# Experts 1 to 6 of a mixture-of-experts kernel: seven block products for the second layer on two pairs of token tiles, in an order written out by hand

## Chip, cores and metric

The kernel runs on one core of a Trainium2 chip. The metric is the time of one execution on the device, in microseconds (us), as the median of the runs shown. The profile is of one execution. TensorE appears in it as PE (products) and PEld (weight loads), VectorE as DVE, ScalarE as ACT, GpSimd as POOL, and the queue that issues the loads from memory as SP.

## The reference, cut to what matters

Strided and local attention gives x, 1152 tokens by 512. A dense mixture of 8 experts follows, whose weights P are balanced by eight rounds over rows and columns (Sinkhorn), and then a mixture that sends each token to two of eight experts.

```python
P = np.exp(logits)
for _ in range(8):
    P /= P.sum(1, keepdims=True) + 1e-09
    P /= P.sum(0, keepdims=True) + 1e-09
    P *= N / E
for e in range(E):                      # 8 experts, w1 512x1024, w2 1024x512
    h = np.maximum(x @ w1[e], 0.0)
    ye = h @ w2[e]
    out += P[:, e:e + 1] * ye
return out.astype(np.float32)
```

The change lies in experts 1 to 6 of the dense mixture, in the end of the balancing, and in what prepares both.

## The kernel before

Every float32 factor of a large product is split in two fp32r parts: ACT writes the high part, DVE the rest (high minus source), and three products (high by high, high by low, low by high) are added in PSUM. `split` does one block of this, `mm3` (L171) the three products.

Attention comes first. Then expert 0 runs in four quarters of its 1024 hidden units, for all nine tiles of 128 tokens (`pair1`, `pair2`); during it the gate logits and all eight rounds of the balancing (`sinkhorn`, L397 to L409) run as a chain of small DVE instructions and one small product a round. GpSimd forms four sums of blocks of x (L683, L685), which `sums` splits in high and low (`sl<-r` on DVE).

Experts 1 to 6 follow in 24 quarters. A quarter is 256 hidden units of one expert. Its 1 MB of weights comes by one load (`fetch_u`, L140). `conv_wino` forms four differences of blocks of w1 on GpSimd (L161) and splits seven blocks; `conv_u2` splits the quarter's part of w2. The first layer is a two by two block product with seven block products (Winograd's form) in place of eight. Class `Unit` does it for a set of columns (tokens): products `p1` to `p7` of six instructions each (L730), sums between them on DVE in PSUM (L751, L755, L761), and relu with a split in gh and gl. Two units, each 288 columns in each half of the tokens, make up the 1152 tokens. The second layer is plain: `pair2` takes one tile of 128 tokens, six products 512 wide (tile y), and DVE adds the result times P to acc (L650); nine tiles make a quarter.

The order of the work on each engine is set by the tile scheduler from the order in which the code is written, except in stretches under `manual_schedule`, where the engine's instructions run as written. Before, the 24 quarters are left to the scheduler, and the stretch after them (expert 7 and the routing) is written by hand. PSUM has eight banks, four tags with two each.

After the quarters come expert 7 (`g1`, `g2`), the routing, and the second mixture (`up`, `Down`), which the change leaves as it is except for when two weight tiles of expert 7 are fetched and split (`load_w`, a0 and b0).

Of the kernel before, what the change touches and what calls it, by code (L numbers as in the profile page):

```python
# [21 lines left out]
NT = N // 128  # L22
# [4 lines left out]
SUB = HALF // 2  # L27
# [35 lines left out]
def tile_kernel(ctx: ExitStack, tc: tile.TileContext, qL, kL, vL, qS, kS, vS, wg, u12, w1, w2, wgn, noise, v1, v2, cst, masks, dummy, out):  # L63
# [91 lines left out]

    def conv_wino(raw):
        hi, lo = (upool.tile([128, 7, 2, 128], F32R, tag=t, name=t) for t in ("u1h", "u1l"))
        t = upool.tile([128, 4, 2, 128], F32, tag="ut", name="ut", bufs=1)
        b11, b21, b12, b22 = (raw[:, 2 * k:2 * k + 2, j * 128:(j + 1) * 128] for j in range(2) for k in range(2))
        for o, x, y in ((0, b12, b11), (2, b22, b12), (1, b22, t[:, 0]), (3, b21, t[:, 1])):  # L160
            nc.gpsimd.tensor_tensor(t[:, o], x, y, op=ALU.subtract)  # L161
        split(hi[:, :2].rearrange("p a b n -> p (a b) n"), lo[:, :2].rearrange("p a b n -> p (a b) n"), raw[:, :, :128])
        split(hi[:, 2], lo[:, 2], b22)
        split(hi[:, 3:], lo[:, 3:], t)
        return hi, lo
# [217 lines left out]
    def sinkhorn():  # L383
        mx = spool.tile([128, 1], F32, name="mx")
        nc.vector.tensor_reduce(mx, lg, axis=AX.X, op=ALU.max)
        p = ps("b", "mxT")
        nc.tensor.transpose(p[:1, :128], mx, ident)
        nmx = spool.tile([1, 1], F32, name="nmx1")
        nc.vector.tensor_reduce(nmx, p[:1, :128], axis=AX.X, op=ALU.max, negate=True)
        p = ps("b", "mxB")  # L390
        nc.tensor.matmul(p[:, :1], onesr[:1, :], nmx, start=True, stop=True)
        nmb = spool.tile([128, 1], F32, name="nmb")
        nc.vector.tensor_copy(nmb, p[:, :1])
        nc.scalar.activation(P.rearrange("p t e -> p (t e)"), lg, AF.Exp, bias=nmb)
        for _ in range(8):
            rs = spool.tile([128, NT], F32, name="rs")
            nc.vector.tensor_reduce(rs, P, axis=AX.X, op=ALU.add)  # L397
            nc.vector.tensor_scalar(rs, rs, 1e-9, None, op0=ALU.add)
            nc.vector.reciprocal(rs, rs)
            nc.vector.tensor_tensor(P, P, rs[:, :, None].to_broadcast([128, NT, E]), op=ALU.mult)  # L400
            c1 = spool.tile([128, E], F32, name="c1")
            nc.vector.tensor_reduce(c1, P.rearrange("p t e -> p e t"), axis=AX.X, op=ALU.add)
            p = ps("b", "cs")
            nc.tensor.matmul(p[:, :E], onesr, c1, start=True, stop=True)
            c2 = spool.tile([128, E], F32, name="c2")
            nc.vector.tensor_scalar(c2, p[:, :E], 1e-9, None, op0=ALU.add)
            nc.vector.reciprocal(c2, c2)
            nc.vector.tensor_scalar(c2, c2, float(N) / E, None, op0=ALU.mult)
            nc.vector.tensor_tensor(P, P, c2[:, None, :].to_broadcast([128, NT, E]), op=ALU.mult)  # L409
# [264 lines left out]
    quarter = [[x[:, 2 * k:2 * k + 2, m * HALF:(m + 1) * HALF] for m in range(2) for k in range(2)] for x in (xh, xl)]  # L674
# [4 lines left out]
    for c in range(2):  # L679
        r = tpool.tile([128, 4, HALF], F32, tag="r", name="r")  # L680
        blocks.append(r)
        for i in range(4):
            nc.gpsimd.tensor_tensor(r[:, i], quarter[0][i][:, c].bitcast(F32), quarter[1][i][:, c].bitcast(F32), op=ALU.add)  # L683
# [19 lines left out]
    with tc.issue_after(marks[1]), tc.issue_after(lows[0].ins):  # L703
        sums()
# [8 lines left out]
    XOP = [(quarter[0][i], quarter[1][i]) for i in (0, 1, 3)] + [(sh[:, i], sl[:, i]) for i in range(4)]  # L713
    A11, A12, A22, S1, S2, S3, S4 = XOP

    class Unit:
        def __init__(self, w, u):
            self.w, self.o = w, u * SUB
            self.bank = {}

        def product(self, k, b, x, first):
            if first:
                self.bank[k] = ps(k, k)
            p = self.bank[k][:, :SUB]
            wh, wl = self.w
            i = 0
            for c in range(2):
                r = [y[:, c, self.o:self.o + SUB] for y in x]
                for l, m in ((wh, r[0]), (wh, r[1]), (wl, r[0])):
# [4 lines left out]
        def keep(self, name, p):  # L734
            s = upool.tile([128, SUB], F32, tag=name, name=name)
            nc.scalar.activation(s, p, AF.Copy)
            return s

        def done(self, p, m, j):
            o = m * HALF + self.o  # L740
            split(gh[:, j, o:o + SUB], gl[:, j, o:o + SUB], p, relu=True)

        def p1(self):
            self.s1 = self.keep("s1", self.product("a", B11, A11, True))

        def p5(self):
            self.s5 = self.keep("s5", self.product("b", T1, S1, True))

        def p6(self):
            p = self.product("a", T2, S2, False)  # L750
            nc.vector.tensor_tensor(self.bank["b"][:, :SUB], p, self.s5, op=ALU.add)  # L751

        def p2(self):
            p = self.product("d", B21, A12, True)
            nc.vector.tensor_tensor(p, p, self.s1, op=ALU.add)  # L755
            self.done(p, 0, 0)

        def p7(self):
            p = self.product("a", T3, S3, False)
            q = ps("c", "c")[:, :SUB]  # L760
            nc.vector.tensor_tensor(q, p, self.s5, op=ALU.add)  # L761
            self.done(q, 1, 1)

        def p3(self):
            self.done(self.product("b", B22, S4, False), 0, 1)

        def p4(self):
            self.done(self.product("a", T4, A22, False), 1, 0)

    tags[:] = ["c", "d"]  # L770
    for_later = []
    for e in range(1, E - 1):
        for q in range(NP):
            raw = fetch_u(e, q)
            a, b = conv_wino(raw[0]), conv_u2(raw[1])
            for u in range(2):
                x = Unit(a, u)
                x.p1()
                x.p5()
                if for_later:  # L780
                    for_later.pop(0)()
                x.p6()
                if for_later:
                    for_later.pop(0)()
                x.p2()
                x.p7()
                for_later = [x.p4, x.p3]
            y = [partial(pair2, b, t, e, past=0 if e == 1 and q == 0 else None) for t in (0, 1, 5, 4, 2, 3, 6, 7, 8)]
            y[0]()
            x.p4()  # L790
            x.p3()
            if e < E - 2 or q < NP - 1:
                for k in range(1, 7):
                    y[k]()
                for_later = y[7:]
    xpair_cm.__exit__(None, None, None)
    wpool = ctx.enter_context(tc.tile_pool(name="wpool", bufs=2, side="right", reuse_waits="tile"))
    a0, b0 = load_w(w1[0, 0]), load_w(w2[0, 0])
    for k in range(1, NT):
        y[k]()  # L800
    gpair_cm.__exit__(None, None, None)
    upool_cm.__exit__(None, None, None)
    tags[:] = ["a", "c"]
    spool = ctx.enter_context(tc.tile_pool(name="late", bufs=2, reuse_waits="tile"))
    shift(spool, 96)
    hpool = ctx.enter_context(tc.tile_pool(name="hpool", bufs=1, reuse_waits="tile"))
# [188 lines left out]
    with tc.manual_schedule(engines=ORDERED):  # L995
        g1(*a0, whole[:2], 0, (0, 1, 2))
# [235 lines left out]
```

## Time and profile before

| | |
|---|---|
| median of 3 runs | 1100.26 us (1098.22 to 1100.57) |
| the profiled execution | 1099.26 us, span 1097.5 us |
| TensorE products busy | 1078.1 us, 98% of the span |
| weight loads busy | 951.0 us, 87% |
| VectorE busy | 657.2 us, 60% |
| ScalarE busy | 397.0 us, 36% |
| GpSimd busy | 183.4 us, 17% |
| mean granted clock of TensorE | 0.994 of full speed |

The span is the part of the execution that the profile covers; 1.76 us lie around it. Busy time of products is modelled, since they are pipelined: the distance from one product's start to the next one's says more than the length of one. A granted clock of 1.00 is TensorE's higher level (2.4 GHz), 0.50 the lower (1.2 GHz).

### The profile page before, as it was taken

How to read it: one execution, taken by the hardware profiler on the slowest of the kernel's cores; microseconds unless marked ns; L12 is line 12 of the kernel's file. 1: busy time of each engine (PE TensorE's matmuls, PEld its weight loads, DVE VectorE, ACT ScalarE, POOL GpSimd, SP SyncE). 2: the span in 40 equal slices, each digit the busy share in tenths (PEclk: the TensorE clock that was granted, in tenths of full speed). 3: DMA queues.
4: the chain of work that ended last, by engine and by line, in shares of the span. 5: the costliest groups of instructions: out<-in, count | busy, mean ns of one | idle time of the engine just before them, and what ended most of it. 6: DMA issues, size and time to landing. Idle time of an engine off the chain costs nothing. (4 is left out here: it accounts for less than half of the span.)

```text
span 1097.5 us, 17182 instructions
## 1 busy us (share of the span) xinstructions
PE 1078.1 (98%) x6840; PEld 951.0 (87%) x6840; DVE 657.2 (60%) x1343; ACT 397.0 (36%) x893; POOL 183.4 (17%) x198
## 2 busy tenths in 40 slices
PE   8999999999999999999999999999999999999996
PEld 5778888999899999889999889988888888888885
DVE  6964886665766666666666666554265565455440
ACT  6741424333322333322332323222123254445541
POOL 2105111111111111121111120010040531233211
PEclk9999999999999999999999999999999999999998
DMA  9321441121111121111121111122103574666531
GB/s 350 135 78 39 131 135 39 39 77 39 40 39 39 41 76 39 39 39 39 39 77 39 39 39 39 39 77 77 39 20 126 164 244 137 207 205 205 186 100 24
DMA packets 31589, 98.18 MB, mean 89 GB/s; under 512 B 6482, under 2 KB 15186, under 8 KB 22928
## 3 DMA queue, kind: packets, MB, share of 16 engines
q1 hardware_dynamic: 16192, 78.94, 19.7%
q0 software_dynamic: 5408, 11.26, 4.8%
q10 hardware_dynamic: 9904, 6.83, 2.0%
q8 instruction: 55, 0.90, 0.3%
q14 instruction: 30, 0.25, 0.1%
HBM read 85.51 MB, written 11.60 MB: 88 GB/s over the span
## 5 line engine op out<-in xcount | busy, mean ns | idle before, releaser
L650 DVE SCALAR_TENSOR_TENSOR acc<-y,P,acc 128x512 f32<-128x512 f32 x207 | 152.8, 748 | 143.4 <-PE y L171 143.3
L171 PE MATMUL y<-u2h,gh 128*128 128x512 f32 x504 | 198.7, 394 | 2.2 <-DVE acc L654 1.9
L171 PE MATMUL y<-u2l,gh 128*128 128x512 f32 x504 | 198.0, 393 | 0.0
L171 PE MATMUL y<-u2h,gl 128*128 128x512 f32 x504 | 189.7, 391 | 0.0
L161 POOL TENSOR_TENSOR ut<-raw 128x256 f32<-128x256 f32 x48 | 34.6, 741 | 489.2 <-DVE u1l L113 457.7
L171 PEld LDWEIGHTS y<-u2h,gl 128*128 128x128 f32 x504 | 94.5, 188 | 19.5
L171 PEld LDWEIGHTS y<-u2h,gh 128*128 128x128 f32 x504 | 94.7, 188 | 19.2 <-DVE acc L654 2.8
L171 PE MATMUL h<-xh,wh 128*128 128x384 f32 (+8 forms) x352 | 109.2, 310 | 0.3 <-DVE hl L109 0.3
L171 PE MATMUL h<-xl,wh 128*128 128x384 f32 (+8 forms) x352 | 109.4, 311 | 0.0
L171 PE MATMUL h<-xh,wl 128*128 128x384 f32 (+8 forms) x352 | 108.8, 309 | 0.0
L171 PEld LDWEIGHTS y<-u2l,gh 128*128 128x128 f32 x504 | 94.6, 188 | 14.2
L108 ACT ACTIVATE hh<-h 128x256 fp32r<-128x256 f32 (+2 forms) x88 | 35.6, 415 | 93.5 <-PE h L171 82.3
L171 PEld LDWEIGHTS h<-xh,wh 128*128 128x128 f32 x352 | 66.2, 188 | 1.1 <-DVE hl L109 0.6
L171 PEld LDWEIGHTS h<-xl,wh 128*128 128x128 f32 x352 | 66.2, 188 | 0.9 <-issue 0.4
L171 PEld LDWEIGHTS h<-xh,wl 128*128 128x128 f32 x352 | 66.2, 188 | 0.0
L111 ACT ACTIVATE u2h<-raw 128x1024 fp32r<-128x1024 f32 x31 | 32.9, 1062 | 90.8 <-PE y L171 90.8
L109 DVE SCALAR_TENSOR_TENSOR hl<-h,hh 128x256 fp32r<-128x256 f32 (+2 forms) x88 | 40.3, 464 | 39.6 <-ACT hh L108 39.6
L113 DVE TENSOR_TENSOR wl<-raw,wh 128x1024 fp32r<-128x1024 f32 x42 | 49.5, 1222 | 22.7 <-ACT wh L111 22.7
L730 PE MATMUL a<-xh,u1h 128*128 128x288 f32 x192 | 56.6, 295 | 0.3 <-DVE acc L654 0.3
L730 PE MATMUL a<-xl,u1h 128*128 128x288 f32 x192 | 56.8, 296 | 0.0
L730 PE MATMUL b<-sh,u1h 128*128 128x288 f32 x192 | 56.7, 295 | 0.0
L730 PE MATMUL a<-sh,u1h 128*128 128x288 f32 x192 | 56.5, 294 | 0.2 <-DVE b L751 0.2
(257 smaller groups left out, 2468.2 us busy)
## 6 DMA issues: line engine op xcount, KB each, us to landing
raw<-in_u SPq DMA_DIRECT2D x31, 1024.0 KB, 4.8
raw<-in_v SPq DMA_DIRECT2D x20, 1024.0 KB, 9.2
acc<-in_v SPq DMA_DIRECT2D x12, 1024.0 KB, 6.9
raw<-in_w SPq DMA_DIRECT2D x4, 1024.0 KB, 5.2
out<-zero ACTq DMA_DIRECT2D x1, 3072.0 KB, 15.5
vs<-in_vL SPq DMA_DIRECT2D x4, 576.0 KB, 7.2
x2d<-acc ACTq DMA_DIRECT2D x9, 256.0 KB, 2.0
vs<-in_vS SPq DMA_DIRECT2D x2, 704.0 KB, 6.9
```

The source lines that it names most:

```text
L108: seen[0] = nc.scalar.activation(hi, src, AF.Relu)
L109: lows.append(nc.vector.scalar_tensor_tensor(lo, src, 0.0, hi.bitcast(F32), op0=ALU.max, op1=ALU.subtract))
L111: seen[0] = nc.scalar.activation(hi, src, AF.Copy)
L113: nc.vector.tensor_tensor(lo, src, hi.bitcast(F32), op=ALU.subtract)
L161: nc.gpsimd.tensor_tensor(t[:, o], x, y, op=ALU.subtract)
L171: nc.tensor.matmul(o, a, b, start=start, stop=stop)
L650: nc.vector.scalar_tensor_tensor(acc[:, t], p, P[:, t, scale:scale + 1], acc[:, t], op0=ALU.mult, op1=ALU.add)
L730: nc.tensor.matmul(p, l[:, b, c], m, start=first and i == 0, stop=i == 5, skip_group_check=not first)
```

## The change

The second layer of a quarter takes tiles 0 and 7, and 1 and 8, as two pairs. For a pair, the two tiles' activations are a two by two block matrix, and so is the quarter's part of w2; class `Two` does the seven block products, each three products 256 wide (L882), and adds each to acc where it belongs. The other five tiles (2 to 6) go as before (`single`, six products 512 wide). For this the units of the first layer become 256 and 320 columns wide (`WIDE`, `AT`): unit 0 holds just the four tiles of the pairs. Its four results are combined by four sums (`mix`, L867 on DVE), and split again (`sums`). The block sums of w2 are formed on GpSimd (`sums2`), and two of the four splits of these blocks have their low part on GpSimd (`pool=True`). The weights come by two loads of 512 KB, one for each layer.

The whole order of the 24 quarters on PE, DVE, ACT and POOL is written out (`quarter`): both units' products alternate, and the last two of the nine tiles go into the next quarter (`rest`). The last two rounds of the balancing (the last column step of round 7 and round 8) move into quarter 0, and the scaling of acc by P of expert 0 becomes an ACT instruction per tile there (`rescale`). The splits of the sums of x (`sums`) are each tied to an earlier instruction, so that they stand apart. w1 of expert 7 is split within the last quarter, w2 after the first part of its first layer.

```diff
-SUB = HALF // 2
+WIDE = (256, 320)
+AT = ((0, 256), (896, 576))
...
     def sums():
-        for c, r in enumerate(blocks):
-            for k, i in enumerate((3, 0, 2, 1)):
-                split(sh[:, k, c], sl[:, k, c], r[:, i])
+        for k, i in enumerate((3, 0, 2, 1)):
+            for c, r in enumerate(blocks):
+                with tc.issue_after(lows[2 * k + c - 12].ins):
+                    split(sh[:, k, c], sl[:, k, c], r[:, i])
...
+        def mix(self, *which):
+            terms = ((3, self.c21, fa[:, 0], ALU.subtract), (0, self.c21, fa[:, 1], ALU.add),
+                     (1, self.c22, us[:, 3], ALU.add), (2, self.c12, us[:, 1], ALU.subtract))
+            for i in which:
+                o, x, y, op = terms[i]
+                nc.vector.scalar_tensor_tensor(us[:, o], x, 0.0, y, op0=ALU.max, op1=op)
...
+    class Two:
+        def product(self, o, a, b, first):
+            h, l = (x[:, a, self.t * 128:(self.t + 1) * 128] for x in ha)
+            r, s = (x[:, b] for x in self.u2)
+            for n, (x, y) in enumerate(((h, r), (h, s), (l, r))):
+                nc.tensor.matmul(o, x, y, start=first and n == 0, stop=n == 2, skip_group_check=not first)
+
+        def add(self, p, t, n):
+            o = acc[:, t, n]
+            nc.vector.scalar_tensor_tensor(o, p, P[:, t, self.e:self.e + 1], o, op0=ALU.mult, op1=ALU.add)
...
-            y = [partial(pair2, b, t, e, past=0 if e == 1 and q == 0 else None) for t in (0, 1, 5, 4, 2, 3, 6, 7, 8)]
...
+    def quarter(n):
...
+        a, b = Two(e, u2, 0, 7, "ab"), Two(e, u2, 1, 8, "dc")
+        if not n:
+            balance_rows()
+            balance_columns("d")
+            balance_rows()
+        run(v.p1, v.p5)
+        if n:
+            lows_of(*ys[:2], x[3], x[2])
...
+        if not last:
+            sums1(n + 1)
+        run(*rest)
+        run(v.p6, v.p2)
+        if not n:
+            balance_columns("d")
+        run(w.p1, v.end2, v.p7)
+        rescale(n, 0, 1)
+        run(v.p3, v.end7)
+        if not n:
+            lows_of(*ys[:2])
...
+        run(w.p5, v.end3, v.p4)
+        v.mix(0, 1)
+        w.p6()
+        v.mix(2, 3)
+        highs(*sums)
+        w.p2()
+        if not last:
+            sums2()
+        run(a.p2, a.p1, w.end2, w.p7)
+        lows_of(sums[0])
+        run(b.p2, b.p1, w.end7, w.p3, w.end3, w.p4)
+        rescale(n, 7, 8, 2)
+        w.end4()
+        lows_of(sums[1])
+        run(a.p5, a.p6, b.p5, b.p6)
...
+        single(e, u2, 2, "b")
+        rescale(n, 3, 4)
+        single(e, u2, 3, "a")
+        lows_of(x[0])
+        run(a.p3, b.p3, a.p7, b.p7, a.end3, b.end3)
...
+            highs(*ys[2:])
+            lows_of(*ys[2:], pool=True)
+            highs(*ys[:2])
...
+        single(e, now, 4, "b")
+        run(a.p4, b.p4)
...
+        rest = [partial(single, e, now, 5, "c"), partial(single, e, now, 6, "d")]
```

On PE, in the second layer of a quarter in the middle of the stretch, before (u2h and u2l are the split w2, gh and gl the split activations, a to d banks of the first layer):

```order
L171 MATMUL y<-u2h,gh 128x512
L171 MATMUL y<-u2l,gh 128x512
L171 MATMUL y<-u2h,gl 128x512
L730 MATMUL a<-xh,u1l 128x288
L730 MATMUL b<-sh,u1h 128x288
L730 MATMUL b<-sl,u1h 128x288
L730 MATMUL b<-sh,u1l 128x288
```

and in the change (hah and hal are unit 0's split activations and their sums, hbh and hbl unit 1's):

```order
L882 MATMUL y<-u2h,hah 128x256
L882 MATMUL y<-u2l,hah 128x256
L882 MATMUL y<-u2h,hal 128x256
L161 MATMUL y<-u2h,hbh 128x512
L161 MATMUL y<-u2l,hbh 128x512
L161 MATMUL y<-u2h,hbl 128x512
```

Four of nine tiles are now done 256 columns at a time.

On DVE during expert 0, where the sums of x are split (sl<-r) beside the additions to acc, before:

```order
L109 SCALAR_TENSOR_TENSOR gl<-h,gh 128x320
L113 TENSOR_TENSOR sl<-r,sh 128x576
L406 TENSOR_SCALAR c_1370<-cs 128x8
L113 TENSOR_TENSOR sl<-r,sh 128x576 x4
L407 RECIPROCAL c_1370<-c_1370 128x8
L113 TENSOR_TENSOR sl<-r,sh 128x576 x2
L654 TENSOR_TENSOR acc<-y,acc 128x512 x2
L113 TENSOR_TENSOR sl<-r,sh 128x576
L654 TENSOR_TENSOR acc<-y,acc 128x512
```

and in the change:

```order
L114 TENSOR_TENSOR sl<-r,sh 128x576
L652 TENSOR_TENSOR acc<-y,acc 128x512 x2
L404 TENSOR_SCALAR c_1370<-cs 128x8
L110 SCALAR_TENSOR_TENSOR gl<-h,gh 128x320
L114 TENSOR_TENSOR sl<-r,sh 128x576
L405 RECIPROCAL c_1370<-c_1370 128x8
L652 TENSOR_TENSOR acc<-y,acc 128x512 x2
```

Seven of the eight stood ahead of two additions to acc; now each has other work before and behind it.

On DVE in quarter 0 of the change (hal takes low parts of unit 0, P and c_2002 belong to the balancing, raw<-a,fa is `mix`):

```order
L398 TENSOR_REDUCE c_1959<-P 128x8
L830 TENSOR_TENSOR b<-a,s_1977 128x256
L834 TENSOR_TENSOR d<-d,s_1968 128x256
L404 TENSOR_SCALAR c_2002<-cs 128x8
L405 RECIPROCAL c_2002<-c_2002 128x8
L406 TENSOR_SCALAR c_2002<-c_2002 128x8
L407 TENSOR_TENSOR P<-P,c_2002 128x72
L816 SCALAR_TENSOR_TENSOR hal<-d,hah 128x256
L843 TENSOR_TENSOR c<-a,s_1977 128x256
L816 SCALAR_TENSOR_TENSOR hal<-c,hah 128x256
L748 TENSOR_TENSOR u2l<-raw,u2h 128x512 x2
L816 SCALAR_TENSOR_TENSOR hal<-b,hah 128x256
```

The balancing's last column step and two low parts of w2 stand here among the first unit's results; from quarter 1 on neither does.

## Rows read from the trace of the kernel before

**Rows 1.** The page's busy times by engine, whole span.

```profile
PE 1078.1 (98%) x6840; PEld 951.0 (87%) x6840; DVE 657.2 (60%) x1343; ACT 397.0 (36%) x893; POOL 183.4 (17%) x198
```

**Rows 2.** Busy by stretch: PE, PEld, DVE, ACT, POOL (instructions), clock, DMA.

```profile
350.00:450.00 100.00, 100.00 (x587) 90.37 (x586) 64.75 (x115) 30.71 (x66) 13.92 (x20) 1.00 0.12 43
```

**Rows 3.** What PE waited for: total us, times, longest us.

```profile
PE y L171 <- DVE acc L654: 1.9, 2, 1.4
...
PE y L171 <- DVE acc L650: 0.3, 1, 0.3
```

**Rows 4.** PE in order of time, products 512 and 288 wide: start, length.

```profile
402.41 0.29 PE L730 MATMUL d<-xh,u1h 128*128 128x288 f32 x1
...
408.35 0.39 PE L171 MATMUL y<-u2h,gh 128*128 128x512 f32 x1
...
409.73 0.29 PE L730 MATMUL b<-sh,u1h 128*128 128x288 f32 x1
```

**Rows 5.** PE in order of time, products 320 wide (expert 0).

```profile
150.78 0.30 PE L171 MATMUL h<-xh,u1h 128*128 128x320 f32 x1
...
152.83 0.31 PE L171 MATMUL h<-xh,u1l 128*128 128x320 f32 x1
```

**Rows 6.** PE in order of time, products 256 wide (second mixture).

```profile
844.89 0.28 PE L171 MATMUL h<-xh,wh 128*128 128x256 f32 x1
...
847.88 0.28 PE L171 MATMUL h<-xl,wh 128*128 128x256 f32 x1
```

**Rows 7.** PE in order of time, around its longest wait.

```profile
133.98 0.40 PE L171 MATMUL y<-u2l,gh 128*128 128x512 f32 x1
135.80 0.50 PE L171 MATMUL y<-u2h,gh 128*128 128x512 f32 x1 [1.42 <-DVE acc L654]
...
136.80 0.39 PE L171 MATMUL y<-u2l,gh 128*128 128x512 f32 x1
137.67 0.60 PE L171 MATMUL y<-u2h,gh 128*128 128x512 f32 x1 [0.48 <-DVE acc L654]
...
138.50 0.47 PE L171 MATMUL h<-xh,u1h 128*128 128x320 f32 x1
...
141.16 0.39 PE L171 MATMUL h<-xl,u1h 128*128 128x320 f32 x1
```

**Rows 8.** Busy by stretch, as rows 2, of one us.

```profile
139.00:140.00 1.00, 1.00 (x5) 1.00 (x5) 0.97 (x4) 0.00 (x0) 0.00 (x0) 0.50 0.95 291
```

**Rows 9.** DVE in order of time, ahead of that wait.

```profile
129.97 3.77 DVE L113 TENSOR_TENSOR sl<-r,sh 128x576 fp32r<-128x576 f32 x4
...
135.07 1.27 DVE L654 TENSOR_TENSOR acc<-y,acc 128x512 f32<-128x512 f32 x2
```

**Rows 10.** PE in order of time, one of three short waits at the quarters' start.

```profile
170.93 0.29 PE L730 MATMUL b<-sh,u1l 128*128 128x288 f32 x1
171.43 0.40 PE L730 MATMUL a<-sh,u1h 128*128 128x288 f32 x1 [0.20 <-DVE b L751]
```

**Rows 11.** Groups by form on DVE: count, busy us, mean ns, idle before.

```profile
L650 DVE SCALAR_TENSOR_TENSOR acc<-y,P,acc 128x512 f32<-128x512 f32 x200 | 147.9, 749 | 140.1 <-PE y L171 140.1
...
L113 DVE TENSOR_TENSOR u1l<-raw,u1h 128x512 fp32r<-128x512 f32 x24 | 16.5, 688 | 12.3 <-ACT u1h L111 12.2
L113 DVE TENSOR_TENSOR u1l<-raw,u1h 128x256 fp32r<-128x256 f32 x24 | 10.1, 419 | 0.0
...
L109 DVE SCALAR_TENSOR_TENSOR gl<-h,gh 128x320 fp32r<-128x320 f32 x8 | 3.9, 484 | 1.8 <-ACT gh L108 1.7
```

**Rows 12.** DVE in order of time, two instructions that wait for nothing.

```profile
407.28 0.45 DVE L109 SCALAR_TENSOR_TENSOR gl<-c,gh 128x288 fp32r<-128x288 f32 x1
407.64 0.45 DVE L109 SCALAR_TENSOR_TENSOR gl<-b,gh 128x288 fp32r<-128x288 f32 x1
```

**Rows 13.** One line's instructions on DVE and POOL: shortest/median/longest ns.

```profile
L113 DVE TENSOR_TENSOR sl<-r,sh x8: 701/746/1292, 129.0 to 136.3; 128x576 fp32r<-128x576 f32 x8
...
L161 POOL TENSOR_TENSOR ut<-raw,ut x48: 732/739/1262, 129.3 to 656.6; 128x256 f32<-128x256 f32 x48
```

More of the change, by code (lines that the diff above doesn't have):

```diff
@@ new lines, in tile_kernel, with fetch1, fetch2, high @@
+    ut = side[:, :2].rearrange("p a n -> p (a n)")
+    vt = pair.tile([128, 4, 256], F32, name="vt")
+    us = side[:, 2:].rearrange("p a (b n) -> p (a b) n", b=2)
+    quarters = [(e, q) for e in range(1, E - 1) for q in range(NP)]
+    def fetch1(n):
+        if n < len(quarters):
+            nc.sync.dma_start((stock[:, :2], spare)[n % 2], u12[quarters[n]][:, :2])
+    def fetch2(n):
+        nc.sync.dma_start(raw2, u12[quarters[n]][:, 2:])
+    def high(hi, src):
+        seen[0] = nc.scalar.activation(hi, src, AF.Copy)
@@ new lines, in single, with rescale @@
+    def single(e, u2, t, bank):
+        p = ps(bank, "y")
+        for k in range(2):
+            h, l = (x[:, k, t * 128 - 256:t * 128 - 128] for x in hb)
+            r, s = (x[:, 2 * k:2 * k + 2].rearrange("p a n -> p (a n)") for x in u2)
+            mm3(p, h, l, r, s, k == 0, k == 1)
+        nc.vector.scalar_tensor_tensor(acc[:, t], p, P[:, t, e:e + 1], acc[:, t], op0=ALU.mult, op1=ALU.add)
+    def rescale(n, *tiles):
+        if n == 0:
+            for t in tiles:
+                nc.scalar.activation(acc[:, t], acc[:, t], AF.Copy, scale=P[:, t, :1])
@@ new lines, in run, with highs, lows_of @@
+    def run(*steps):
+        for s in steps:
+            s()
+    def highs(*blocks):
+        for hi, lo, src in blocks:
+            high(hi, src)
+    def lows_of(*blocks, pool=False):
+        for hi, lo, src in blocks:
+            low(hi, lo, src, pool)
+    fetch1(0)
+    fetch2(0)
+    sums1(0)
+    sums2()
+    x = first_weights(0)
+    highs(*x)
+    lows_of(*x)
+    fetch1(1)
+    u2, ys = second_weights()
+    highs(*ys)
+    lows_of(*ys[2:], pool=True)
+    wpool = a0 = None
+    rest = []
@@ L804, in tile_kernel @@
+    with tc.manual_schedule(engines={mybir.EngineType.PE, mybir.EngineType.DVE, mybir.EngineType.Activation, mybir.EngineType.Pool}):
+        for n in range(len(quarters)):
+            quarter(n)
+        run(*rest)
+        lows_of(*x[2:])
+    pair_cm.__exit__(None, None, None)
+    raw_b = fetch_w(w2[0, 0])
     spool = ctx.enter_context(tc.tile_pool(name="late", bufs=2, reuse_waits="tile"))
     shift(spool, 96)
+    tags[:] = ["a", "c"]
     hpool = ctx.enter_context(tc.tile_pool(name="hpool", bufs=1, reuse_waits="tile"))
@@ L995, in tile_kernel @@
     with tc.manual_schedule(engines=ORDERED):
-        g1(*a0, whole[:2], 0, (0, 1, 2))
+        g1(*a0, whole[:2], 0, (0,))
+        b0 = conv_w(raw_b)
+        g1(*a0, whole[:2], 0, (1, 2))
         a1 = conv_w(raws[0])
```

256 lines of the change are left out of this document (172 added, 84 removed).

## The prediction

> **What bounds the kernel now.** I read the busy times first, then the stretches, the waits of TensorE, and its order in time. TensorE is at work for 98% of the span and VectorE for 60% [rows 1]. In the 24 quarters of experts 1 to 6 it is 100%, at the higher clock level throughout [rows 2]: nothing there waits for a load, and time can be won only by fewer or cheaper products, or lost by a wait that isn't there yet. TensorE's waits on other engines come to a few us in the whole kernel [rows 3], and the longest stand just ahead of the quarters. So the questions are what the products cost by width, whether VectorE keeps up, and what becomes of those waits.
>
> What a product costs is the distance between starts. Products 512 wide: six from 408.35 to 409.73, 0.230 us each; 288 wide: 45 from 402.41 to 408.35, 0.132 [rows 4]. 320 wide: 14 from 150.78 to 152.83, 0.1464 [rows 5]. 256 wide: 25 from 844.89 to 847.88, 0.1196 [rows 6]. A check: by these prices a quarter of 84 products of 288 and 54 of 512 takes 11.09 + 12.42 = 23.51 us; 587 products started in 100 us [rows 2] are 138 in 23.5 us.
>
> **The change, part by part.**
>
> *Products.* First layer: 42 of 256 and 42 of 320 in place of 84 of 288, 5.02 + 6.15 = 11.17 us (0.08 more). Second layer: a pair takes 21 products 256 wide in place of 12 of 512; two pairs 42 x 0.1196 = 5.02, five single tiles 30 x 0.230 = 6.90, 11.92 in place of 12.42. A quarter falls to 23.09 us, 0.42 less; 24 quarters give **-10.1 us**. The pairs pay as long as a narrow product costs less than 24 x 0.230 / 42 = 0.131 us; at 0.1196 there is a tenth to spare.
>
> The Trainium skill speaks against this: TensorE: Matmul & The Clock Gate, section Back-to-back issue gap, gives about 81 ns for a product 128 wide and about 131 ns for one 512 wide in a stream with weight loads. An estimate on a line between these, 98 ns at 256, would make the two layers 0.98 us a quarter dearer, 24 us in all. Rows 4 and 6 disagree (230 and 119.6 ns); the measurement decides.
>
> *VectorE.* Per quarter it gets three sums and three low parts of 256 for unit 0, four for mix, ten additions of 256 and two of 512 for the pairs, three sums and four low parts of 320 for unit 1, five additions of 512 for single tiles, seven low parts of 512 and one of 256 between SBUF tiles: 42 instructions. With 0.42, 0.48, 0.75, 0.69 and 0.42 us [rows 11] (for 256 wide I take the SBUF row for all) the lengths sum to 20 x 0.42 + 7 x 0.48 + 7 x 0.75 + 7 x 0.69 + 0.42 = 22.3 us. Neighbours overlap: starts lie 0.36 apart where each is 0.45 long [rows 12], so 42 x 0.09 = 3.8 come off: 18.5 us of 23.09, 80%. Before, 14 of 0.455, nine of 0.75 and 3.55 of splits gave 14.2 of 23.5. VectorE stays below TensorE, but its spare time halves.
>
> I walked the written queues of one quarter with these distances. The nearest place is unit 1's fourth product: it adds into a bank that VectorE must first have read for the sum after the seventh. In between TensorE has two products of a pair and the third of unit 1, 6 x 0.1196 + 6 x 0.1464 = 1.6 us, and VectorE is through with about half a us left. The chain from mix over ScalarE's high and VectorE's low part to the pair's fifth product takes some 4.5 us, where TensorE has 5.8 of other work ahead. So I put nothing for the 23 later quarters, with 0.3 us each (7 us) as the upper end.
>
> *GpSimd.* Its share rises from four differences to eight plus two low parts of 512: 8 x 0.74 + 2 x 1.48 = 8.9 us a quarter, off the path. It matters only where it slows VectorE: a split of a sum of x between SBUF tiles took 1.29 us at worst in place of 0.70, and a GpSimd difference at the same time 1.26 in place of 0.74 [rows 13]. Eight of VectorE's 42 are of that kind, 5.25 us. If half of them meet GpSimd at 1.84 times their price, VectorE gains 2.2 us, to 20.7: still below 23.09.
>
> *Splits spread.* Before, six splits and one small instruction fill VectorE from 129.97 to 135.07 ahead of two additions to acc [rows 9]. TensorE stands for want of a bank: 133.98 to 135.80 and 136.80 to 137.67, less 0.23 for the product itself, 1.59 + 0.64, and 0.1 between [rows 7]. Then the granted clock is 0.50, the lower level [rows 8], from about 137.7 to 141.2: ten products of 320 from 138.50 to 141.16 take 2.66 us in place of 1.46, and the two before them lose 0.4. With the splits behind the additions in the queue both go: **-2.3 and -1.6**. Bounds: nothing (the stall only moves) and these 3.9.
>
> *Short waits* where quarters start and end: three between 165 and 172 us, of 0.2 to 0.45 us by the starts around them (171.43 less 170.93 less 0.13 is 0.37 [rows 10]), and one of 0.3 for a bank near 725 [rows 3]: **-1.3**, because the written order puts other products there; zero is the other bound.
>
> *Quarter 0.* The balancing's end puts about 13 small instructions and two low parts of w2, beside GpSimd's, on VectorE ahead of mix, and the pair's first product needs a bank that mix still reads. No row shows this wait. It lies between nothing and the 1.59 us of rows 7, which also brought 1.6 us of halved clock. I take 1.2, nearer the long row since VectorE's queue is as full there, without the clock: **+1.2**.
>
> *Rest.* Two loads of 512 KB in place of one of 1 MB ask for a quarter's weights a quarter ahead; nothing waits. SP holds the first layer's load behind the second's, both due over 15 us later. ScalarE, 31% busy [rows 2], gets some seven more instructions a quarter, hidden behind the products. At the end, w2 of expert 7 is split inside its first layer: **+0.5**. Unknown handovers between the three kinds of product, which before never alternated so: between 0 and 2, taken as **+0.7**.
>
> *Sum.* -10.1 - 3.9 - 1.3 + 1.2 + 0.5 + 0.7 = -12.9. The profiled execution took 1099.26 us (1097.5 of span and 1.76 around it), 1.0 below the median of the runs, 1100.26. So 1086.4 for it, and **1087.4 us** for the median.
>
> **The rivals.**
>
> *VectorE has no margin, now and then.* If half a us in unit 1's banks is lost to GpSimd, TensorE waits 0.2 to 0.5 us a quarter, 5 to 12 us: 1092 to 1099. For it: the spare time halves, and eight of VectorE's instructions can meet GpSimd; against it: most of them read PSUM, and such additions ran in 0.75 us through the whole stage. 0.18.
>
> *VectorE becomes the bound* (slower). It decides from 23.6 us of VectorE a quarter, where 0.53 x 24 eats the 12.9. With half the overlap (20.4) and nearly all two-SBUF instructions slowed (3.6) a quarter takes 24.0, 0.91 above TensorE: 22 us, 1109. For it: the lengths alone sum to 22.3; against: rows 12 show the overlap. 0.09.
>
> *The waits before the quarters only move.* Quarter 0 holds TensorE as long as rows 7 did and the clock halves again: 4 us come back, 1091. 0.14.
>
> *Narrow products cost more here*, the mechanism of the page's rule, because the weight load of each is not covered. The loads' busy time over their count is 951.0 / 6840 = 0.139 us [rows 1]; at that price the 84 narrow products add 84 x 0.0194 = 1.6 us a quarter, 39 us: 1126. Rows 6 show 0.1196 in the same form. 0.02.
>
> *The change doesn't do what it says*: TensorE's order is fixed by hand, the rows of the order show the narrow products, so the arithmetic cannot stay away; 0.
>
> **How the numbers follow.** Forecast as summed, 1084 to 1090: 0.57. The first rival 0.18, the third 0.14, the slower one 0.09, the fourth 0.02. About 0.2% (2.2 us) is what a measurement of this kernel can tell from no change. Faster: the forecast, the third rival and most of the first, 0.86. Within 0.2%: 0.03. Slower: 0.11. The range runs from 1083.5 (all gains, no new wait: -15.3, and 1.5 us of scatter between runs) up to 1097.5, which takes in most of the first rival.
>
> **What would show it.** In the profile after: 256-wide products 0.12 us apart; a quarter in 23.1 us; no wait and no lower clock between 130 and 142 us; VectorE busy about 80% in the quarters without a wait of TensorE on it; one wait near 165 us, of about 1 us. Wrong would be a wait of TensorE on VectorE that comes back in each quarter, VectorE without idle time, or products 256 wide further apart than 0.131 us.

## The result, and the profile after

The changed kernel takes **1086.87 us** (median of 4 runs, 1085.41 to 1088.33) against 1100.41 us for the kernel before in the same runs: ratio 0.9882, 95% interval 0.9869 to 0.9896. The forecast was 1087.4 us. The profiled execution took 1086.06 us, its span is 1084.2.

Busy time by engine on the page of the changed kernel, which answers to [rows 1]:

```profile
PE 1066.0 (98%) x7272; PEld 964.0 (89%) x7272; DVE 774.9 (71%) x1705; ACT 454.4 (42%) x1063; POOL 313.7 (29%) x346
```

Busy by stretch, columns as in [rows 2]: the twelve us that held the long stall of [rows 7], and a hundred us of quarters.

```profile
130.00:142.00 12.00, 12.00 (x68) 10.85 (x67) 9.42 (x24) 3.33 (x6) 3.40 (x4) 1.00 0.12 35
350.00:450.00 100.00, 100.00 (x684) 95.04 (x683) 86.10 (x182) 43.25 (x103) 36.27 (x44) 1.00 0.14 46
```

The stall and the halved clock of [rows 7, 8] are gone: TensorE is busy for all twelve us at a clock of 1.00. In the quarters TensorE still has no idle time, but VectorE is now busy for 86 of 100 us instead of 65, GpSimd for 36 instead of 14.

TensorE in order of time in quarter 10 (start, length), as [rows 4, 6]: the first of twelve products 256 wide, the first of twelve 512 wide, and the product behind them.

```profile
404.94 0.28 PE L882 MATMUL y<-u2h,hah 128*128 128x256 f32 x1
...
406.38 0.40 PE L161 MATMUL y<-u2h,hbh 128*128 128x512 f32 x1
...
409.13 0.28 PE L882 MATMUL y<-u2h,hah 128*128 128x256 f32 x1
```

Twelve narrow products take 1.44 us, 0.120 each; twelve wide ones 2.75, 0.229 each. The length of a quarter is read from VectorE's first sum of unit 0, which comes once in each:

```profile
394.72 0.43 DVE L830 TENSOR_TENSOR b<-a,s 128x256 f32<-128x256 f32 x1
417.82 0.43 DVE L830 TENSOR_TENSOR b<-a,s 128x256 f32<-128x256 f32 x1
```

23.10 us, where the prediction had 23.09. What TensorE waited for (total us, times, longest), as [rows 3]; shown are three rows, those of the attention stage and of the rest of the kernel are left out:

```profile
PE y L161 <- DVE hl L110: 1.6, 1, 1.6
...
PE y L882 <- DVE raw L867: 1.1, 1, 1.1
...
PE y L882 <- DVE acc L886: 0.4, 1, 0.4
```

The first stands in expert 7, the other two in quarter 0. In quarters 1 to 23 this view shows no wait of TensorE.

To see where the time went I cut both spans where the quarters begin and where expert 7 begins. The rows are TensorE's first products there, before and then after:

```profile
159.97 0.29 PE L730 MATMUL d<-xh,u1h 128*128 128x288 f32 x1
...
728.00 0.33 PE L171 MATMUL h<-xh,wh 128*128 128x384 f32 x1
```

```profile
158.86 0.28 PE L796 MATMUL a<-xh,u1h 128*128 128x256 f32 x1
...
715.71 0.33 PE L161 MATMUL h<-xh,wh 128*128 128x384 f32 x1
```

Before, the scheduler had put 15 products of expert 0 behind the first of these rows (3.4 us) and six of the last quarter behind the second (1.4 us), so its cuts are 163.4 and 729.4.

| stage | before | after | difference | predicted |
|---|---|---|---|---|
| up to the quarters | 163.4 | 158.9 | -4.5 | -3.9 |
| the quarters | 566.0 | 556.8 | -9.2 | -9.5 (-10.1 - 1.3 + 1.2 + 0.7) |
| expert 7 and the rest | 368.1 | 368.5 | +0.4 | +0.5 |
| span | 1097.5 | 1084.2 | -13.3 | -12.9 |

### The profile page after: what moved, and what is told of

Read it like the earlier page. It is cut to its first block, busy times and chain, and to the rows that moved or that the text cites. A ratio compares the mean times of both kernels' runs of the same rounds, so it can differ in the third digit from the quotient of the medians.

```text
span 1084.2 us, 18865 instructions
## 1 busy us (share of the span) xinstructions
PE 1066.0 (98%) x7272; PEld 964.0 (89%) x7272; DVE 774.9 (71%) x1705; ACT 454.4 (42%) x1063; POOL 313.7 (29%) x346
## 5 line engine op out<-in xcount | busy, mean ns | idle before, releaser
L886 DVE SCALAR_TENSOR_TENSOR acc<-y,P,acc 128x256 f32<-128x256 f32 (+1 forms) x288 | 135.7, 519 | 0.0
L882 PE MATMUL y<-u2h,hah 128*128 128x256 f32 x336 | 94.9, 282 | 1.5 <-DVE raw L867 1.1
L882 PE MATMUL y<-u2h,hal 128*128 128x256 f32 x336 | 95.1, 283 | 0.0
L882 PE MATMUL y<-u2l,hah 128*128 128x256 f32 x336 | 95.1, 283 | 0.0
L161 PE MATMUL y<-u2h,hbh 128*128 128x512 f32 x240 | 94.3, 393 | 0.0
L161 PE MATMUL y<-u2l,hbh 128*128 128x512 f32 x240 | 94.2, 393 | 0.0
L161 PE MATMUL y<-u2h,hbl 128*128 128x512 f32 x240 | 93.4, 389 | 0.0
L926 DVE SCALAR_TENSOR_TENSOR acc<-y,P,acc 128x512 f32<-128x512 f32 x120 | 85.3, 743 | 0.6 <-PE y L161 0.6
L882 PEld LDWEIGHTS y<-u2h,hah 128*128 128x128 f32 x336 | 64.0, 190 | 4.1 <-issue 1.3
L882 PEld LDWEIGHTS y<-u2l,hah 128*128 128x128 f32 x336 | 64.0, 190 | 1.8
L882 PEld LDWEIGHTS y<-u2h,hal 128*128 128x128 f32 x336 | 64.3, 191 | 0.0
```

Source lines behind the costliest of these rows:

```text
L161: nc.tensor.matmul(o, a, b, start=start, stop=stop)
L882: nc.tensor.matmul(o, x, y, start=first and n == 0, stop=n == 2, skip_group_check=not first)
L886: nc.vector.scalar_tensor_tensor(o, p, P[:, t, self.e:self.e + 1], o, op0=ALU.mult, op1=ALU.add)
L926: nc.vector.scalar_tensor_tensor(acc[:, t], p, P[:, t, e:e + 1], acc[:, t], op0=ALU.mult, op1=ALU.add)
```

## The experiments

**Theory**: the products give some 10 us, the stall and the halved clock before the quarters some 4, and VectorE has a little room left. **Rivals**: the gain comes from the new order and the spread splits, and the pairs bring little; or VectorE already bounds the quarter. All runs were timed against the kernel before on the same chip. The profiles show one more thing that matters in reading the ratios: expert 7's stage, whose code is nearly the same in all these kernels, took between 366.1 and 371.8 us (last section), and the medians contain that. The start varies too: one and the same product of expert 0, well ahead of the stall, begins at 101.42 us before, at 101.44 in the change, and between 101.1 and 102.9 in the other profiles. So the length of a quarter, read as above, and the time from that product to the beginning of expert 7 decide wherever they can.

### The splits alone, in the kernel before (e1)

```diff
-        for c, r in enumerate(blocks):
-            for k, i in enumerate((3, 0, 2, 1)):
-                split(sh[:, k, c], sl[:, k, c], r[:, i])
+        for k, i in enumerate((3, 0, 2, 1)):
+            for c, r in enumerate(blocks):
+                with tc.issue_after(lows[2 * k + c - 12].ins):
+                    split(sh[:, k, c], sl[:, k, c], r[:, i])
...
-    with tc.issue_after(marks[1]), tc.issue_after(lows[0].ins):
+    with tc.issue_after(marks[0]):
         sums()
```

> The kernel before, with nothing of the change but the splits of the sums of x spread one by one behind single low parts of expert 0. Theory: the stall near 134 to 138 us and the halved clock behind it go (2.3 + 1.6 us by the rows of before), nothing else changes: 1096 to 1097 us, ratio 0.996 to 0.997, and a quarter stays at 23.5 us. Rival (the gain of the change comes mainly from the order, the products matter little): 1090 us or less. Other rival (the stall only moves): 1100, and a wait of the same length elsewhere before 175 us.

Measured: 1097.38 us, a little above the range; ratio 0.9975 (0.9966 to 0.9984). The stretch of the stall (columns as above):

```profile
130.00:142.00 12.00, 12.00 (x69) 10.90 (x68) 10.01 (x24) 3.71 (x7) 3.36 (x4) 1.00 0.47 158
```

Full, at full clock: the stall does not move, it goes. Expert 7 begins at 725.30 us instead of 728.00, 2.7 earlier, although TensorE came later to the same product of expert 0, which lies ahead of the edit's place (before, then here):

```profile
101.42 0.42 PE L171 MATMUL h<-xh,u1h 128*128 128x320 f32 x1
```

```profile
102.88 0.42 PE L171 MATMUL h<-xh,u1h 128*128 128x320 f32 x1
```

From this product to expert 7 the kernel is 4.2 us shorter (622.4 in place of 626.6), the whole of the 3.9 that was expected. The ratio shows only 2.7 us, a fifth of the change: the profiled execution (1098.16 us, 0.8 above the median) lost 1.5 us ahead of this product and 1.6 in expert 7's stage (last section), where the edit changes nothing. The rival that the products matter little falls.

### The change without the spread splits (e2)

The opposite edit, in the changed kernel.

> The changed kernel with the eight splits of the sums together again, behind the same marks as before. Theory: the stall of TensorE comes back with its halved clock, 2 to 4.5 us more than the change: 1089 to 1091.5 us; quarters 1 to 23 stay at 23.10 us. Rival (Sinkhorn's later end, which now reaches into quarter 0, already took the pressure off VectorE): within 0.5 us of the change, 1087, without a wait over 0.5 us before quarter 0.

Measured: 1089.04 us, ratio 0.9905 (0.9889 to 0.9920), 2.2 us more than the change. The same stretch, and TensorE's wait in quarter 0:

```profile
130.00:142.00 12.00, 11.38 (x61) 9.42 (x60) 11.90 (x24) 5.93 (x12) 3.51 (x4) 1.00 0.96 288
```

```profile
PE y L881 <- DVE raw L866: 1.5, 1, 1.5
```

VectorE is full in this stretch again (11.90 of 12) and TensorE stands, but only for 0.6 us, and the clock stays at 1.00. The quarters begin 1.0 us later (159.84), quarter 0 waits 0.4 more, expert 7 begins at 717.16, 1.45 later (its own stage took 2.2 more, 370.7 us). Counted from the same product of expert 0 (101.13 here) it is 1.8. So the splits are worth 1.8 us here and 4.2 in the kernel before: the price of a stall belongs to the place it has in the order, and the halved clock came only with the longer one. The halved clock that was expected here did not come.

### The change without the pairs (e3)

The tiles of unit 0 are computed as the other tiles are, at the same places of the order.

```diff
-        v.mix(0, 1)
+        v.end4()
         w.p6()
-        v.mix(2, 3)
-        highs(*sums)
         w.p2()
-        run(a.p2, a.p1, w.end2, w.p7)
-        lows_of(sums[0])
-        run(b.p2, b.p1, w.end7, w.p3, w.end3, w.p4)
+        tile(0, "a")
+        run(w.end2, w.p7)
+        tile(1, "d")
+        run(w.end7, w.p3, w.end3, w.p4)
...
-        run(a.p5, a.p6, b.p5, b.p6)
+        tile(7, "b")
+        tile(8, "c")
```

> The changed kernel with the four tiles of unit 0 computed by six products 512 wide each, in the same places of the order; mixing sums, their high and low parts and the sums of w2 are left out, the result is the same. Theory (price of products): four tiles cost 24 x 0.2295 = 5.51 us in place of 42 x 0.1197 = 5.03, so a quarter takes 23.58 in place of 23.10, 11.5 us in all, less up to 1.8 us of quarter 0's waits, which hang on VectorE: 1096.5 to 1098.5. Rival (the written order and the spread splits bring the gain, and the pairs only load VectorE): within 2 us of the change, 1085 to 1089.

Measured: 1099.84 us, ratio 0.9999 (0.9990 to 1.0008). TensorE's first product of two neighbouring quarters:

```profile
393.23 0.28 PE L796 MATMUL a<-xh,u1h 128*128 128x256 f32 x1
```

```profile
416.86 0.28 PE L796 MATMUL a<-xh,u1h 128*128 128x256 f32 x1
```

23.63 us a quarter, 0.53 more than the change, 0.05 more than I expected (the third product of a quarter, which reads a split of w1, starts 0.1 us late). The quarters run from 159.28 to 726.82 us, 567.5 in all against 556.8: 10.7 us are what the pairs bring, 24 x 0.53 less the waits of quarter 0, which this kernel does not have. The median lies above the range because expert 7's stage took 371.8 us here, 3.7 more than in the kernel before. Up to expert 7 this kernel is 2.6 us ahead of that one (726.8 against 729.4; 3.0 from the same product of expert 0, which starts at 101.86 here). The rival falls: order and splits bring about 3 us of the 13.3, the pairs most of the rest.

### More work for VectorE in the full stretch (e4)

```diff
     def low(self, p, m, j):
...
-            nc.vector.scalar_tensor_tensor(l, p, 0.0, h.bitcast(F32), op0=ALU.max, op1=ALU.subtract)
+            for _ in range(1 + self.u):
+                nc.vector.scalar_tensor_tensor(l, p, 0.0, h.bitcast(F32), op0=ALU.max, op1=ALU.subtract)
```

> The changed kernel in which VectorE writes each of unit 1's four low parts of 320 twice, the same values again: about 4 x 0.40 = 1.6 us more of VectorE a quarter, 21.7 of 23.1. Theory (VectorE has room but for half a us at unit 1's fourth product): TensorE waits there by some of the 1.6 that stand ahead of it, 0 to 0.5 us a quarter, so 1087 to 1099 with a period of 23.1 to 23.6. Rival (VectorE already bounds the quarter): the whole 1.6 us appear in each period, 24.7 us, 1125 us.

Measured: 1133.02 us, ratio 1.0301 (1.0287 to 1.0315). Here my theory fell, and the time lies above the rival's 1125 too. VectorE's first sum in two quarters, and TensorE's two longest waits in total:

```profile
389.82 0.42 DVE L831 TENSOR_TENSOR b<-a,s 128x256 f32<-128x256 f32 x1
414.81 0.42 DVE L831 TENSOR_TENSOR b<-a,s 128x256 f32<-128x256 f32 x1
```

```profile
PE y L161 <- DVE hbl L817: 8.7, 24, 0.7
PE y L883 <- DVE acc L887: 8.0, 23, 0.8
```

A quarter takes 25.0 us, 1.9 more, for 1.6 us of added work. The waits come once in each quarter, at two places behind unit 1's low parts. How much VectorE works in one whole quarter shows in these rows (columns as above), of the change and of this run:

```profile
394.72:417.82 23.10, 23.10 (x159) 21.86 (x158) 20.13 (x43) 9.88 (x23) 8.35 (x11) 1.00 0.14 46
```

```profile
389.82:414.81 24.99, 24.25 (x159) 22.03 (x158) 22.51 (x47) 9.76 (x23) 8.79 (x11) 1.00 0.14 46
```

VectorE is busy 2.38 us longer and idle for 2.48 us in place of 2.97. That it works longer than the doubled work accounts for comes from this meeting of VectorE and GpSimd (each in order of time):

```profile
402.32 1.48 DVE L748 TENSOR_TENSOR hal<-raw,hah 128x512 fp32r<-128x512 f32 x1
```

```profile
401.95 1.30 POOL L748 TENSOR_TENSOR u2l<-vt,u2h 128x512 fp32r<-128x512 f32 x1 [7.61 <-ACT u2h L745]
...
403.20 1.75 POOL L748 TENSOR_TENSOR u2l<-vt,u2h 128x512 fp32r<-128x512 f32 x1
```

VectorE's subtraction of two SBUF tiles takes 0.68 us alone, 1.48 here: it starts 0.37 behind GpSimd's and ends 0.55 behind that one's end (403.25). Then GpSimd's second one ends 1.15 behind VectorE's end and takes 1.75 instead of 1.30. In the changed kernel VectorE's comes before GpSimd's in quarters 1 to 23; the added work pushed it into it.

### The same, with GpSimd's two instructions moved away (e7)

```diff
-            lows_of(*ys[2:], pool=True)
             highs(*ys[:2])
...
             sums1(n + 1)
+        if n:
+            lows_of(*ys[2:], pool=True)
         run(*rest)
```

> The run with four doubled low parts (1133 us), and GpSimd's two low parts of w2's sums moved from behind ScalarE's high parts to the next quarter, behind the sums of w1. Theory: its 1.92 us a quarter are 1.6 of doubled work, 0.8 because VectorE's low part of the mixing sums met GpSimd (1.48 in place of 0.68), less half a us of room; without the meeting 1.1 us a quarter stay, 1133 less 19: 1112 to 1117. Rival (the meeting hides in idle time, the room was simply gone): within 4 us of 1133.

Measured: 1115.18 us, ratio 1.0140 (1.0123 to 1.0158), as expected.

```profile
406.38 0.42 DVE L831 TENSOR_TENSOR b<-a,s 128x256 f32<-128x256 f32 x1
430.57 0.42 DVE L831 TENSOR_TENSOR b<-a,s 128x256 f32<-128x256 f32 x1
```

A quarter takes 24.2 us: 0.8 less for one VectorE instruction that meets nobody. VectorE's work in this quarter:

```profile
406.38:430.57 24.19, 23.85 (x159) 21.97 (x158) 21.71 (x48) 9.76 (x23) 8.27 (x11) 1.00 0.13 43
```

It is 1.58 us more than in the change, and the quarter is 1.09 longer: the room is 0.5, as it was with the meeting (2.38 less 1.89).

### Half as much work, inside the stretch and in gaps (e6; e5, e9, e12)

Inside the stretch, two doubled low parts of unit 1 (e6):

```diff
-        run(b.p2, b.p1, w.end7, w.p3, w.end3, w.p4)
+        run(b.p2, b.p1, w.end7, w.end7, w.p3, w.end3, w.end3, w.p4)
```

> The changed kernel with two of unit 1's low parts of 320 written twice, 0.8 us more of VectorE a quarter, as much as the run with the extra work in gaps, but inside the stretch that has no idle time. Theory: 0.8 less the half a us that VectorE has left, 0.3 us a quarter, 1092 to 1096 us; more, up to 0.3 + 0.8 = 1.1 us a quarter (1113), if the low part of the mixing sums then meets GpSimd's two of w2 and takes 1.48 in place of 0.68. Rival (VectorE's sum decides): the same time as the run with the extra work in gaps.

Measured: 1092.19 us, ratio 0.9931 (0.9919 to 0.9943), and

```profile
397.72 0.42 DVE L830 TENSOR_TENSOR b<-a,s 128x256 f32<-128x256 f32 x1
421.04 0.42 DVE L830 TENSOR_TENSOR b<-a,s 128x256 f32<-128x256 f32 x1
```

23.32 us, 0.22 more. VectorE's work in this quarter rose from 20.13 us by 0.72, so the room is again 0.5:

```profile
397.72:421.04 23.32, 23.32 (x158) 21.92 (x157) 20.85 (x46) 9.87 (x23) 8.35 (x11) 1.00 0.14 45
```

In gaps, three tries. The first (e5) doubled a low part and the sum for unit 0's sixth product:

```diff
+            if self.u == 0:
+                nc.vector.tensor_tensor(self.bank["b"][:, :self.w], self.bank["a"][:, :self.w], self.s5, op=ALU.add)
...
-        run(v.p3, v.end7)
+        run(v.p3, v.end2, v.end7)
```

> The changed kernel with two more VectorE instructions of 256 in each quarter, the same values again: unit 0's sum after its sixth product and its low part after the second, both where VectorE stands for 0.72 us waiting for ScalarE's high part; about 0.8 us more of VectorE a quarter (20.0 to 20.8 of 23.1). Theory (the place decides: only the stretch from unit 1's second low part to the quarter's end is full): 0 to 0.1 us a quarter, 1086 to 1089 us. Rival (VectorE's sum over the quarter decides, as four extra instructions cost 1.9 us a quarter): 0.5 to 0.8 us a quarter, 1099 to 1106.

Measured: 1094.31 us, ratio 0.9947 (0.9933 to 0.9960), between the two ranges; a quarter takes 23.32 us, just as inside the stretch, which looks as if the sum decided. But unit 0's seventh product writes bank a, which the doubled sum reads until 399.48, and it started late:

```profile
399.26 0.31 PE L796 MATMUL a<-xh,u1l 128*128 128x320 f32 x1
399.54 0.39 PE L796 MATMUL a<-sh,u1h 128*128 128x256 f32 x1
```

0.28 between two starts where 0.147 is usual, and 0.22 to the next one (399.76) where 0.12 is: 0.23 in all, the whole of what the quarter lost. The dose had made its own wait. The second try (e9) put a low part of w1 in the sum's place:

```diff
         run(v.p6, v.p2)
+        if n:
+            lows_of(x[3])
```

> As the run with extra work in gaps, but with instructions that no product waits for: unit 0's low part after the second product again, behind the sum for its seventh, and the low part of w1's block B22 again, behind unit 0's sum after the second product; about 0.8 us more of VectorE a quarter in two gaps of 0.72. In the first try the doubled sum read bank a, and unit 0's seventh product waited for that reading by 0.14 us and a slower start. Theory (place decides): a quarter stays at 23.10 us within 0.05, 1086 to 1088.5 us in all. Rival (VectorE's sum over the quarter decides): again 0.2 to 0.3 us a quarter, 1092 to 1095.

Measured: 1121.97 us, ratio 1.0216 (1.0201 to 1.0230). The added low part stands behind the next load into the same buffer, so it computes block B22's low part from other weights, and TensorE waited 27.0 us in 21 waits for it. It says nothing of the question.

The third (e12) doubled only low parts that nothing waits for:

```diff
-        run(v.p3, v.end7)
+        run(v.p3, v.end2, v.end7)
...
-        run(w.p5, v.end3, v.p4)
+        run(w.p5, v.end3, v.end7, v.p4)
```

> The changed kernel with two of unit 0's low parts of 256 written twice where VectorE stands: the second product's, behind the sum for the seventh (a gap of 0.72 us), and the seventh's, behind the third's (a gap of 0.41); about 0.7 us more of VectorE a quarter, and no product or load waits for either. Theory (place decides): a quarter within 0.05 of 23.10 us, 1086 to 1088.5 us, ratio 0.987 to 0.989. Rival (VectorE's sum over the quarter decides): 0.2 us a quarter as for the doubled low parts inside the full stretch, 1091.5 or more, ratio 0.992 or more.

Measured: 1084.80 us, ratio 0.9878 (0.9861 to 0.9894), the change's own ratio; the median lies below the range, in runs in which the kernel before took only 1097.81 us and expert 7's stage here 366.3. One whole quarter, and the period:

```profile
395.35:418.45 23.10, 23.10 (x159) 21.86 (x158) 20.79 (x44) 9.88 (x23) 8.38 (x11) 1.00 0.13 46
```

```profile
395.35 0.43 DVE L830 TENSOR_TENSOR b<-a,s 128x256 f32<-128x256 f32 x1
418.45 0.43 DVE L830 TENSOR_TENSOR b<-a,s 128x256 f32<-128x256 f32 x1
```

VectorE is busy 0.66 us longer, almost as much as in e6, and the quarter is 23.10 us to the hundredth. The place decides, not the sum.

### Quarter 0 in another order (e8, e10, e11)

In the changed kernel quarter 0's two waits are these (TensorE, in order of time), and ahead of the first VectorE and GpSimd meet as above:

```profile
167.59 0.31 PE L796 MATMUL d<-xh,u1l 128*128 128x320 f32 x1
168.98 0.35 PE L882 MATMUL y<-u2h,hah 128*128 128x256 f32 x1 [1.08 <-DVE raw L867]
...
179.92 0.40 PE L161 MATMUL y<-u2h,hbl 128*128 128x512 f32 x1
180.75 0.39 PE L882 MATMUL y<-u2h,hah 128*128 128x256 f32 x1 [0.43 <-DVE acc L886]
```

```profile
165.53 1.75 POOL L748 TENSOR_TENSOR u2l<-vt,u2h 128x512 fp32r<-128x512 f32 x1
```

```profile
166.05 1.79 DVE L748 TENSOR_TENSOR u2l<-raw,u2h 128x512 fp32r<-128x512 f32 x1
```

First try (e8): one of VectorE's two splits of w2 goes behind mix, and GpSimd's low parts behind its sums of w1.

```diff
-            lows_of(*ys[:2])
+            lows_of(ys[1])
...
         v.mix(2, 3)
+        if not n:
+            lows_of(ys[0])
```

> The changed kernel with quarter 0 put in another order: of w2's first-half splits only the one that the first pair product reads stands ahead of mix, the other behind it; and GpSimd's two low parts of w2's sums come behind its sums of w1. Theory: the wait of 1.08 us near 168 us (1.24 with the handover) goes, as VectorE's splits no longer meet GpSimd's ahead of mix (1.2 down to 0.7 each); the one of 0.43 near 180 us stays or goes: 1085 to 1086 us. Rival (the wait only moves to the next instruction that VectorE then is late for): within 0.5 us of 1086.9, a wait of about 1 us at another place before 182 us.

Measured: 1088.17 us, ratio 0.9898 (0.9885 to 0.9911); expert 7 begins at 715.94 us, 0.2 later than in the change (0.3 earlier from the same product of expert 0, 102.01 here), and its stage took 370.5, which puts the median above both ranges. The rival's wait came:

```profile
170.09 0.39 PE L882 MATMUL y<-u2l,hah 128*128 128x256 f32 x1 [0.98 <-DVE u2l L748]
```

The pair's second product follows the first at once and reads the split that I had put last. Second try: that split right behind mix's first two.

```diff
-            lows_of(*ys[:2])
-            fetch2(n + 1)
-            fetch1(n + 2)
+            lows_of(ys[1])
         run(w.p5, v.end3, v.p4)
         v.mix(0, 1)
+        if not n:
+            lows_of(ys[0])
+            fetch2(n + 1)
+            fetch1(n + 2)
         w.p6()
```

With GpSimd's low parts late in every quarter (e10) and in quarter 0 alone (e11):

> The changed kernel with GpSimd's two low parts of w2's sums moved in every quarter behind the sums of w1 (as in the run with four doubled low parts and that move), and in quarter 0 one of w2's first-half splits ahead of mix and the other right behind mix's first two, ahead of the sum after unit 1's sixth product (not behind mix's last two, where the pair's second product stood 0.98 us for it). Theory: quarter 0's two waits, 1.84 us in all, fall to 0.3 or less: span 1082 to 1083.5, median 1085.0 to 1086.3. Rival (they only move again): a wait of 0.5 us or more between 165 and 185 us, 1086.5 to 1088.

> The same as the run before it, but GpSimd's low parts come late in quarter 0 alone. Theory: the first wait of quarter 0 is gone as there; the one near 180 to 183 us, where VectorE's split of w1 met GpSimd (1.48 in place of 0.68), stays with 0.4 us: 0.2 to 0.6 us slower than that run. Rival (meetings of this kind hide in VectorE's idle time in quarter 0): the same time.

Measured: 1083.56 us, ratio 0.9863 (0.9845 to 0.9881), and 1083.95 us, ratio 0.9868 (0.9851 to 0.9884). By the ratios that is 2.1 and 1.5 us better than the change, though the intervals overlap its own; both beat the kernel before clearly, and both medians lie below their ranges. But quarter 0 gives little of it: e10 still waits once, for 0.85 us, as its rival had it, because VectorE's moved split now met GpSimd's moved low part and took 1.73 us:

```profile
167.53 1.73 DVE L748 TENSOR_TENSOR u2l<-raw,u2h 128x512 fp32r<-128x512 f32 x1
```

It reaches expert 7 at 715.23 us, 0.5 earlier than the change. The other 2.0 of its shorter span (1081.7) come in expert 7's stage, 366.5 us instead of 368.5, where the edit changes nothing. e11 lost its first wait but kept one of 0.5 where VectorE's split of w1 met GpSimd (1.51 us), and began the quarters later (159.72); that GpSimd's place matters for the time of quarter 0 is neither shown nor excluded by a difference of 0.4 us.

## Why the prediction was right, and where it was off

**Products.** The main term held: -10.1 predicted, 24 x (23.51 - 23.10) = -9.8 by the prediction's own 23.51 for before and the measured 23.10, and the run without pairs shows that it is the pairs that bring it. The rule that the prediction weighed against its rows, from the Trainium skill, TensorE: Matmul & The Clock Gate, section Back-to-back issue gap, would by its two figures have made the layers dearer; the trace disagrees, 0.120 us at 256 and 0.229 at 512 in the changed kernel's own stream.

**Splits spread.** -3.9 predicted for stall and clock, -4.5 for the stage in the profile after. That the edit alone does it is shown, with 4.2 us in the kernel before; but in the changed one it is worth 1.8, and without it the stage, counted from the same product of expert 0, is already 3.3 us shorter than before (58.7 against 62.0). So much of the gain comes with the rest of the change as well, and the terms were not independent. Which part does it, the end of the balancing that moved to quarter 0 or another, no run separates.

**Quarter 0.** +1.2 predicted, 1.24 for the first wait (168.98 less 167.59 less 0.15) and 0.60 for a second one that I had not foreseen (180.75 less 179.92 less 0.23). The clock stayed at 1.00, as forecast. The size of the first was luck: it was chosen between nothing and 1.59, not worked out, and the split that meets GpSimd took 1.79 us where the longest of [rows 13] is 1.29.

**Short waits and handovers.** Besides 24 times their period the quarters took 1.8 us before (566.0 - 564.2) and 2.4 after (556.8 - 554.4), of which quarter 0's two waits make 1.84. So the short waits of before are gone and were nearer 1.8 than 1.3, and of the 0.7 for handovers at most 0.6 shows. The two terms together came out 0.6 us better than summed, about what the second wait of quarter 0 cost: that the total fits so well is in part luck.

**VectorE.** Two numbers were mis-sized. Its busy time is 20.13 us a quarter, not 18.5: I took 0.09 us of overlap off all 42 instructions, while those that start after a gap, some ten, have none, and the ten additions of 256 from PSUM take 0.474 and not 0.42; this makes up most of the difference. The rows could have told: the same reckoning gave 14.2 us before, where [rows 2] show 0.6475 x 23.51 = 15.2. And the point from which the slower rival decides was wrong: I put it at 23.6 us of VectorE a quarter, but 22.51, with the added work in the wrong place, make the quarter 25.0 us. What counts is the stretch from unit 1's second low part to the next quarter's first sum, 402.62 to 417.82 us in the profile after: 15.2 us with one gap worth naming, of 0.32. Its room is 0.5 us, the "half a us" that the prediction gave for unit 1's fourth product alone; outside the stretch 0.7 us cost nothing. So the rival with VectorE as the bound was nearer than its 0.09 says: four more instructions of 0.4 us in that stretch made it true (e4).

**GpSimd.** The prediction priced a meeting at 1.84 times VectorE's duration. The rows show turns: whichever starts first finishes, and the other ends 0.55 us (VectorE) or 1.15 (GpSimd) behind that end, a little under its own length. The Trainium skill, SBUF — State Buffer, section Who interferes with whom, states that an instruction of VectorE with two SBUF inputs contends with one of GpSimd that reads SBUF, and calls the contention an exclusive lock; the trace agrees. If the lock lasts for the whole instruction, as these turns suggest, the worst price of a meeting is an estimate of GpSimd's 1.30 us on top of 0.68; the longest here took 1.79. In quarters 1 to 23 of the change no meeting happened to fall into the stretch.

**The end.** +0.5 predicted, +0.4 measured for the stage, but this is no proof of the term: the stage varies by more than that with edits elsewhere, and TensorE's wait of 1.6 us in it is one that e10 to e12 do not have.

## What to carry to other kernels

Ask of an engine that is nearly full not how much idle time it has in a period, but how much there is between the places where others wait for it: here 3 us idle in 23 came down to 0.5 us of room. Where a VectorE instruction with two SBUF inputs stands in such a stretch, place GpSimd's large instructions so that they cannot start ahead of it even when it comes a little late. And when adding work to measure room, add instructions whose operands nobody is about to overwrite, or the dose makes its own wait.

## What the runs showed of the hardware that was not expected

VectorE stood in expert 7's stage for lengths that changed with edits in other stages, often without a releaser that the profile shows. It is the same stretch of the program in all kernels; in order of time, the changed kernel, in which the product that needs the next low part stands for 1.57 us behind this:

```profile
799.55 0.18 DVE L536 TENSOR_TENSOR rk<-rank,cs 128x24 f32<-128x24 f32 x1 [1.31 <-remote]
```

the first try at quarter 0:

```profile
806.09 0.75 DVE L436 SCALAR_TENSOR_TENSOR acc<-y,P,acc 128x512 f32<-128x512 f32 x1 [5.42 <-remote]
```

the same addition in the run with four doubled low parts, where the profile names a small product of TensorE:

```profile
850.59 0.75 DVE L436 SCALAR_TENSOR_TENSOR acc<-y,P,acc 128x512 f32<-128x512 f32 x1 [4.69 <-PE cnt L607]
```

and in e10, where it only waits for its product:

```profile
800.50 0.75 DVE L436 SCALAR_TENSOR_TENSOR acc<-y,P,acc 128x512 f32<-128x512 f32 x1 [0.59 <-PE y L161]
```

In all eight runs e1 to e8 VectorE is idle for 4.7 to 5.4 us ahead of this addition and for 2.8 to 3.5 ahead of the next, and the stage took 369.2 to 371.8 us; TensorE then waits 1.8 to 2.6 us for a low part. Before, in the change and in e9 to e12 these gaps are 0.6 and 2.0 us, and the stage took 366.1 to 368.5. A load of instructions falls into this stretch with the long gap (801 us in e8) and without it (800 us in e10), so it does not tell them apart. The cause stays open; it means that a difference of 2 us between two medians here needs a look at this stage before it is put down to an edit.
